# Splitting a broadcast load into two DMAs of 64 partitions, with a list schedule's constants set anew

## The chip, the cores and the metric

The kernel runs on one core of a Trainium2 chip. The core has five engines, each working through its own queue in order: TensorE (matrix products, PE in the profile, with its weight loads as PEld), VectorE (DVE), ScalarE (ACT), GpSimd (POOL) and SyncE (SP, which here only issues DMAs). Sixteen DMA engines move data between HBM and the on-chip memory. The metric is the device time of one execution in microseconds.

## The reference

Three layers stand in series. The change lies in the first.

```python
def phi(x):                                     # features, 64 -> 2 * 128
    proj = np.einsum('bhsd,df->bhsf', x, w_phi)
    proj = proj - np.max(np.abs(proj), axis=-1, keepdims=True)
    return np.concatenate([np.exp(proj), np.exp(-proj)], axis=-1)
q_p, k_p = phi(q), phi(k)                       # q, k, v: (4, 8, 576, 64)
kv = np.einsum('bhsf,bhsd->bhfd', k_p, v)
z = np.sum(k_p, axis=2)
num = np.einsum('bhsf,bhfd->bhsd', q_p, kv)
den = np.einsum('bhsf,bhf->bhs', q_p, z)[..., None] + 1e-06
x = num / den                                   # -> 2304 tokens x 512
h = np.maximum(x @ w_in, 0); x = h * h @ w_out  # 512 -> 2048 -> 512
# then a layer of 8 experts (512 -> 1024 -> 512), each weighted per token by
# a softmax of x @ w_gate that is normalised 8 times along rows and columns
```

`w_in` and `w_out` arrive as 64-bit floats. The kernel reads them as pairs of 32-bit integers and decodes them on VectorE.

## The kernel before

**Attention.** The 4 x 8 heads are handled as 16 units of two heads each (NU = 16; unit `u` is batch `u // 4` and head pair `u % 4`). The two heads of a unit lie on partitions 0 to 63 and 64 to 127. The steps of a unit, with their names in the planner: loads of k, q and v (`ldk`, `ldq`, `ldv`, SP); transposes (`tk`, `tq`, TensorE) and copies (`kc`, `qc`, ScalarE); the feature projection of k (`pk`), its peak and shift (`mkp`, `mkr`, `sup`, `sur`, VectorE) and the two exponentials (`en`, `ep`, ScalarE); the sums over the tokens (`A`, TensorE), a copy and a transpose (`kvs`, `kvt`), `kvc` and the reduction for z (`zs` on VectorE, `zw`, a copy, on GpSimd); the same features for q in two halves (`pq`, `ec`, the absolute maximum over all partitions `par` on GpSimd, `qs`, `qn`, `qp`); the numerators `psn` and the denominators `psd` (TensorE).

**The reciprocal and its way.** A unit has 2 x 576 denominators. `dn` (ScalarE) copies them out of the accumulator, `cmp` (a DMA) spreads them over 128 partitions with 9 each, `rec` (VectorE) takes the reciprocals, `rd` (a DMA) writes them to a small array `rden` in HBM, and `rb` (a DMA) reads them back so that each partition of a head holds all 576 values of that head. The source of this DMA is 2 heads x 64 copies (step 0) x 576 values, and the target 128 partitions. `mul` (VectorE) multiplies the numerators by them. `xhi` (GpSimd) and `xlo` (VectorE) split the product into a high and a low part, `xh` and `xl`, the input of the next layer. The tile `rb` exists once, so `rb` of a unit waits for `mul` of the unit before.

**The first pass of the second layer** is mixed into the same stage. Its weights are decoded in 12 blocks of 7 VectorE steps (`op`; blocks 0, 2, 4 and 6 for the first pass, two tiles each, 8 to 15 for the second, one tile each) and split (`sh`, `sl`). Of its eight groups of 288 tokens, six have their first product (`L1`) in the plan and five their second (`L2`); results go to HBM (`od`, the store `part<-o`). Each of these products is 12 matmuls, since a product of two split numbers takes three.

**What sets the order.** Lines 287 to 397 are a list scheduler that runs on the host when the kernel is built. Each step has an engine, a duration (us), the steps that it needs, the accumulator banks that it takes and frees, and a key. The scheduler goes through time; on each engine it picks, of the steps that are ready, the one with the smallest key. The key of an attention step is its unit's base, `EARLY * min(u, 5) + LATE * max(0, u - 5)`, plus `PHASE[name]`; that of a decode block is `DUE[block]` (first loads: `RAW`); the products of the second layer have keys of 10,000 and more, so they fill what is left; steps with no key get their ready time plus `SOON`. DMAs are priced as one issue (`ISSUE`, 0.63 us), 1 us, `kb / 195` us (in order, one after another) and 0.25 us. The scheduler's result fixes only the order in which each engine's instructions are issued. The times on the chip come from the hardware.

Nearly all instructions of the stage are recorded through two helpers, so that they carry line 104 (VectorE, ScalarE, GpSimd and SP) or line 224 (TensorE); tile names tell them apart. `psw`, `pss`, `pskt` are accumulators of the attention, `ps` of the second layer; `ek` and `eq` are features of k and q, `nm` the numerators, `dm` and `wf` tiles of the decode.

**After the stage** come the rest of the first pass, three further passes and the expert layer. None of their code is touched.

Of the kernel before, what the change touches and what calls it, by code (L numbers as in the profile page):

```python
# [20 lines left out]
def tile_features_attention__moe__sinkhorn_moe(  # L21
# [20 lines left out]
    B, H, S, D = q.shape  # L42
# [3 lines left out]
    NE, _, FE = w1.shape  # L46
# [25 lines left out]
    ep = early.enter_context(tc.tile_pool(name="early", bufs=1, side="right", reuse_waits="tile"))  # L72
# [7 lines left out]
    rden = dram.tile([NU, T2], F32, name="rden")  # L80
# [30 lines left out]
    A = InOrder(nc.scalar, "act")  # L111
# [157 lines left out]
    def first_l2(g, t0, n, dst=None, pool=None, cols=range(KD)):  # L269
# [15 lines left out]
    S_ = InOrder(nc.sync, "sp")  # L285

    LAT = {"PE": 0.30, "DVE": 0.07, "ACT": 0.07, "POOL": 0.10, "SP": 0.07}
    RINGS = {"w": 2, "s": 2, "m": 2}
    EARLY, LATE = 12.97, 18.72
    PHASE = {  # L290
        "ldk": -41.9, "ldq": -26.4, "ldv": -12.4, "tq": 0.3, "qc": -8.6, "tk": -5.8, "kc": -29.8, "pk": 1.3,
        "mkp": -19.8, "sup": -1.2, "mkr": -3.5, "sur": -14.7, "en": -3.0, "ep": -6.7, "A": 4.4, "kvs": 20.1,
# [3 lines left out]
        "rb": 13.8, "mul": 6.0, "xhi": 38.2, "xlo": 39.8, "ldw": -30.9,  # L296
    }
    START = {"PE": 2.2, "DVE": 2.2, "ACT": 3.0, "POOL": 9.0, "SP": 0.8}

    ISSUE = 0.63  # L300
    SOON = 1.33
    SLACK = {"PE": 0.4, "DVE": 0.1, "ACT": 0.1, "POOL": 0.1, "SP": 0.0}
    FREELY = "ws"
    class Step:
# [8 lines left out]
    def add(name, eng, dur, emit, needs=(), after=(), takes=(), frees=(), key=0.0, kb=0, cols=0):  # L313
        steps[name] = Step(
            name, eng, dur, emit, [n for n in needs if n], [n for n in after if n], takes, frees, key, kb, cols
        )

    def schedule():
# [34 lines left out]
        while len(made) < len(steps):  # L353
# [30 lines left out]
            for u, whole in s.users:  # L384
                u.ready = max(u.ready, s.end if whole else s.start)
                u.left -= 1
                if u.key is None:
                    u.key = s.end + SOON
                if not u.left:
# [10 lines left out]
    def attention(u):  # L400
# [3 lines left out]
        def n(nm, v=u):  # L404
            return f"{nm}{v}" if 0 <= v < NU else None
# [3 lines left out]
        def step(nm, *args, **how):  # L409
            add(n(nm), *args, key=base + PHASE[nm], **how)  # L410
# [50 lines left out]
        def k_peak(c):  # L461
            def emit():
                ps = x["ps" + c]
                mk = x["mk", c] = ab.tile([P, ps.shape[1], 1], F32, tag="mk" + c, bufs=1, name="mk")
                V.tensor_reduce(mk, ps, AX.X, ALU.max, apply_absolute_value=True)

            return emit

        def k_shift(c):
            def emit():  # L470
                if c == "p":
                    x["ek"] = ab.tile([P, 2 * MT + 1, 2, NF], F32, tag="ek", bufs=1, name="ek")
                ps, ek = x["ps" + c], x["ek"]
                to = ek[:, : 2 * MT, 0] if c == "p" else ek[:, 2 * MT :, 0]
                V.tensor_sub(to, ps, x["mk", c].to_broadcast(list(ps.shape)))

            return emit

        def k_exp(sign):
            ek = x["ek"]  # L480
            A.activation(ek[:, :, 1 if sign < 0 else 0], ek[:, :, 0], AF.Exp, scale=float(sign))

        step("pk", "PE", 1.15, proj_k, [n("kc"), "ldw"], [n("A", u - 1)], ("w", "s"), ([n("sup")], [n("sur")]), cols=2)
        step("mkp", "DVE", 1.23, k_peak("p"), [n("pk"), n("sup", u - 1)])
        step("mkr", "DVE", 0.29, k_peak("r"), [n("pk"), n("sur", u - 1)])
        step("sup", "DVE", 1.23, k_shift("p"), [n("mkp"), n("A", u - 1)])
        step("sur", "DVE", 0.29, k_shift("r"), [n("mkr"), n("sup"), n("A", u - 1)])
        step("en", "ACT", 1.02, lambda: k_exp(-1), [n("sup"), n("sur")])
        step("ep", "ACT", 1.02, lambda: k_exp(1), [n("en")])

        def rows(i, h):
            return x["ek"][:, 2 * MT if i == MT else MT * h + i].rearrange("p a f -> p (a f)")
# [42 lines left out]
        step("kvt", "PE", 0.40, kvt, [n("kvs")], [], ("m",), ([n("kvc"), n("zs")],))  # L535
        step("kvc", "ACT", 0.37, kvc, [n("kvt"), n("psn", u - 1)])
        step("zs", "DVE", 0.17, zs, [n("kvt"), n("zw", u - 1)])
        step("zw", "POOL", 0.44, zw, [n("zs"), n("psd", u - 1)])

        x["psq"] = [None, None]  # L540

# [26 lines left out]
        def of(function, *args):  # L568
            return lambda: function(*args)

        for c in range(2):
            step(f"pq{c}", "PE", 0.52, of(proj_q, c), [n("qc"), "ldw"], [n("psd", u - 2)], ("w",), ([n(f"ec{c}_")],), cols=2)
            step(f"ec{c}_", "ACT", 0.64, of(q_copy, c), [n(f"pq{c}"), n("psn", u - 2), n("psd", u - 2)])
            step(f"par{c}_", "POOL", 2.26, of(q_peak, c), [n(f"ec{c}_")])
            step(f"qs{c}_", "DVE", 0.85, of(q_shift, c), [n(f"par{c}_")])
            step(f"qn{c}_", "ACT", 0.68, of(q_exp, c, -1), [n(f"qs{c}_")])
            step(f"qp{c}_", "ACT", 0.68, of(q_exp, c, 1), [n(f"qn{c}_")])
# [42 lines left out]

        def to_rows():
            t = x["rb"] = ab.tile([P, S], F32, tag="rb", bufs=1, name="rb")
            S_.dma_start(t, rden[u].rearrange("(j o s) -> j o s", j=2, o=1).to_broadcast([2, D, S]))

        ts_ = slice(b * S, (b + 1) * S)

# [11 lines left out]
        )  # L638
        step("psd", "PE", 1.13, denominators, [n("qp0_"), n("qp1_"), n("zw")], [n("psn")], ("s",), ([n("dn")],), cols=1)
        step("nm", "ACT", 0.65, nm, [n("psn"), n("xlo", u - 2), n("xhi", u - 2)])  # L640
        step("dn", "ACT", 0.4, dn, [n("psd"), n("cmp", u - 1)])
        step("cmp", "SP", ISSUE, to_comp, [n("dn"), n("rd", u - 1)], kb=20)
        step("rec", "DVE", 0.22, recip, [n("cmp")])
        step("rd", "SP", ISSUE, to_dram, [n("rec")], kb=20)
        step("rb", "SP", ISSUE, to_rows, [n("rd"), n("mul", u - 1)], kb=230)
        step("mul", "DVE", 0.83, mul, [n("rb"), n("nm")])
        raws_of = []
        step("xhi", "POOL", 1.0, xhi, [n("mul")] + raws_of)
        step("xlo", "DVE", 0.86, xlo, [n("xhi")] + raws_of)

    def load_wphi():
        S_.dma_start(wphi, w_phi.rearrange("(o d) f -> o d f", o=1).to_broadcast([2, D, NF]))
# [2 lines left out]
    for u in range(NU):  # L655
        attention(u)

    def decoding(j, wide):
# [37 lines left out]
        for d in range(c):  # L696
            add(
                f"ldr{j + d}", "SP", ISSUE, load(d),
                [f"ldr{j + d - 1}" if j + d else None, f"op{prev}_5" if j == 6 or j > 8 else None]
                + (["ldq0"] if j + d == 0 else []) + [], key=RAW.get(j, due - 5) + d / 10, kb=512,  # L700
            )
# [18 lines left out]
            add(f"sh{j}", "ACT", 1.05, sh, [f"op{j}_6"], key=due + 8)  # L720
            add(f"sl{j}", "DVE", n / 960 + 0.15, sl, [f"sh{j}"], key=due + 9)

    RAW = {0: -31.09, 2: -7.57, 4: 30.41, 6: 29.03}
    DUE = {
        0: 19.8, 2: 58.2, 4: 67.3, 6: 90.9, 8: 117.7, 9: 126.3, 10: 134.8, 11: 143.4, 12: 151.9, 13: 160.5,
        14: 169.0, 15: 177.6,
    }
    for j in range(0, 8, 2):
        decoding(j, True)
# [609 lines left out]
    for n in range(NN):  # L1339
        l2 = layer2(n)  # L1340
        if n + 1 < NN:
            l1 = layer1(n + 1)
            p, q = order[n + 1]
# [75 lines left out]
```

## Time and profile before

| | |
|---|---|
| median of 3 runs (range) | 2108.54 us (2107.21 to 2110.11) |
| profiled execution: time, span | 2110.18 us, 2108.4 us |
| TensorE busy | 2040.1 us (97%) |
| VectorE, ScalarE, GpSimd busy | 1670.2, 827.9, 810.8 us |
| mean granted TensorE clock | 0.986 |
| DMA | 375.12 MB, mean 178 GB/s |

The span runs from the first to the last instruction. All times in rows are microseconds from the span's start, or durations, unless they say ns. "Busy" of TensorE is the time in which matmuls are in flight by a model of their ends. PEclk is the granted clock as a share of full speed, 1.00 being 2.4 GHz. In a group's row, what stands after the bar is the time that the engine sat idle just before such instructions, with what ended most of it. The chain of waits is followed back from the last instruction, at each step to what released it; "SPq" is SP's queue.

### The profile page before, as it was taken

What the parts mean: (1) busy time and instruction counts of PE and PEld (TensorE: products, weight loads), DVE (VectorE), ACT (ScalarE), POOL (GpSimd) and SP (SyncE); (2) the same over time, 40 slices, a digit from 0 to 9 for tenths busy, and PEclk for the clock granted to TensorE, in tenths of its full rate; (3) what the DMA queues carried; (4) which work ended last, traced back from release to release, by engine and by line L of the source; (5) the groups of instructions that cost most, each with busy time, mean ns of one, the idle gap of its engine ahead of it and who ended that gap; (6) DMA issues with size and microseconds to landing.
All of it is one profiled execution on the core that took longest, in us unless ns stands there. A gap on an engine that the chain in (4) does not pass through costs nothing.

```text
span 2108.4 us, 31244 instructions
## 1 busy us (share of the span) xinstructions
PE 2040.1 (97%) x12427; PEld 1922.3 (91%) x12427; DVE 1670.2 (79%) x1910; ACT 827.9 (39%) x1240; POOL 810.8 (38%) x457
## 2 busy tenths in 40 slices
PE   7888879999999999999999999999999999999998
PEld 4466559888899999999999999999999999999998
DVE  6657433757456798999989989889898998988986
ACT  5655433222233654333433334333333333333332
POOL 3323310323102644443544444444444444444431
PEclk9889989999999999999999999999999999999999
DMA  5434213101134566667676676676766666676663
GB/s 146 102 97 111 73 38 94 61 30 51 40 123 169 228 225 216 215 219 253 222 229 220 215 252 223 222 232 214 243 226 225 229 222 231 224 229 233 212 202 121
DMA packets 180643, 375.12 MB, mean 178 GB/s; under 512 B 71058, under 2 KB 110866, under 8 KB 180498
## 3 DMA queue, kind: packets, MB, share of 16 engines
q1 hardware_dynamic: 180498, 373.12, 53.2%
q8 instruction: 99, 1.62, 0.3%
q14 instruction: 46, 0.38, 0.1%
HBM read 348.67 MB, written 24.34 MB: 177 GB/s over the span
## 4 chain that ended last, share of the span: by engine, by line
PE 84%; DMA 7%; DVE 6%; issue 1%; SPq 1%; ACT 1%; POOL 0%; DVEq 0%; ACTq 0%; POOLq 0%
PE psa L1160 31%; PE psb L1160 31%; PE ps L224 18%; DMA rb<-rden 5%; PE psw L224 2%; PE pss L224 2%; SPq L104 1%; DMA xl<-xv 1%; DVE acc L1276 1%; DVE xl L896 1%; PE psg L937 1%; DVE r L1228 0%; DVE w2v L896 0%; DVE nm L104 0%; DMA rden<-comp 0%
## 5 line engine op out<-in xcount | busy, mean ns | idle before, releaser
L1160 PE MATMUL psa<-xl,xh 128*128 128x384 f32 x2400 | 447.0, 335 | 3.6 <-DVE xl L896 2.5
L1160 PE MATMUL psb<-xl,xh 128*128 128x384 f32 x2400 | 445.0, 334 | 2.0 <-DVE acc L1276 0.7
L1160 PEld LDWEIGHTS psa<-xl,xh 128*128 128x128 f32 x2400 | 419.7, 188 | 4.7 <-DVE xl L896 2.9
L1160 PEld LDWEIGHTS psb<-xl,xh 128*128 128x128 f32 x2400 | 418.1, 188 | 3.2 <-issue 1.7
L1188 POOL TENSOR_TENSOR t<-r,r 128x768 f32<-128x768 f32 x96 | 207.1, 2157 | 503.7 <-DVE r L1228 457.9
L1188 POOL TENSOR_TENSOR t<-r,t 128x768 f32<-128x768 f32 x96 | 236.0, 2458 | 7.4 <-ACT r L1232 1.9
L896 DVE TENSOR_TENSOR xl<-t,xl 128x768 fp32r<-128x768 f32 x128 | 186.8, 1460 | 1.9 <-ACT xl L895 1.7
L1276 DVE TENSOR_TENSOR acc<-psa,acc 128x768 f32<-128x768 f32 x161 | 152.9, 950 | 40.0 <-PE psa L1160 36.4
L1276 DVE TENSOR_TENSOR acc<-psb,acc 128x768 f32<-128x768 f32 x163 | 154.8, 950 | 37.0 <-PE psb L1160 33.7
L1160 PE MATMUL psb<-xl,w2v 128*128 128x384 f32 x960 | 180.3, 334 | 0.0
L1160 PE MATMUL psa<-xl,w2v 128*128 128x384 f32 x960 | 180.2, 334 | 0.0
L895 ACT CAST xl<-t 128x768 fp32r<-128x768 f32 x128 | 107.1, 837 | 155.5 <-POOL t L1188 65.5
L1160 PEld LDWEIGHTS psb<-xl,w2v 128*128 128x128 f32 x960 | 167.6, 188 | 0.0
L1160 PEld LDWEIGHTS psa<-xl,w2v 128*128 128x128 f32 x960 | 167.6, 188 | 0.0
L895 ACT CAST xl<-r 128x768 fp32r<-128x768 f32 x96 | 80.4, 838 | 155.8 <-PE psa L1160 79.2
L224 PE MATMUL ps<-xh,w0h 128*128 128x288 f32 (+3 forms) x384 | 133.9, 349 | 4.1 <-ACT o L104 3.8
L896 DVE TENSOR_TENSOR xl<-r,xl 128x768 fp32r<-128x768 f32 x96 | 132.4, 1379 | 1.4 <-ACT xl L895 1.4
L224 PE MATMUL ps<-xl,w0h 128*128 128x288 f32 (+3 forms) x384 | 131.5, 342 | 0.0
L224 PE MATMUL ps<-xh,w0l 128*128 128x288 f32 (+3 forms) x384 | 131.2, 342 | 0.0
L224 PE MATMUL ps<-gl,w1h 128*128 128x288 f32 (+3 forms) x384 | 129.5, 343 | 0.0
L224 PE MATMUL ps<-gh,w1l 128*128 128x288 f32 (+3 forms) x384 | 128.6, 341 | 0.0
L969 POOL TENSOR_TENSOR s<-wf 128x512 f32<-128x512 f32 x32 | 44.6, 1393 | 212.6 <-DVE xvs L896 80.6
(198 smaller groups left out, 3585.7 us busy)
## 6 DMA issues: line engine op xcount, KB each, us to landing
xl<-xv SPq DMA_DIRECT2D x329, 768.0 KB
wf<-in_moe_w_dram SPq DMA_DIRECT2D x32, 1024.0 KB
gate<-prT SPq DMA_DIRECT2D x45, 384.0 KB
xv<-xvs SPq DMA_DIRECT2D x14, 768.0 KB
raw<-in_moe_w_in_dram SPq DMA_DIRECT2D x16, 512.0 KB
raw<-in_moe_w_out_dram SPq DMA_DIRECT2D x16, 512.0 KB
xv<-xl SPq DMA_DIRECT2D x7, 768.0 KB
rb<-rden SPq DMA_DIRECT2D x16, 288.0 KB
```

Of the source, the lines that this page charges most:

```text
L104: ins = made(*args, **how)
L224: latest["pe"] = op(*args, **how).ins
L895: nc.scalar.copy(v[:, 0], src)
L896: nc.vector.tensor_sub(v[:, 1], src, v[:, 0].bitcast(F32))
L937: ins = nc.tensor.matmul(ps[:, t], accT[:, k, t0 + t * P : t0 + (t + 1) * P], wg[:, k], start=first is None, stop=k == KD - 1, skip_group_ ...
L969: nc.gpsimd.tensor_tensor(s1, a(2, 1), a(2, 2), ALU.add)
L1160: ins = nc.tensor.matmul(ps[:, x, :NB], w[:, wi, k, cs], b[:, bi, k], start=first and k + i == 0, stop=k == KH - 1 and i == 2, skip_group_ ...
L1188: nc.gpsimd.tensor_tensor(t[nm], x, y, ALU.subtract)
L1276: latest["dve"] = nc.vector.tensor_add(o, ps, o).ins
```

## The change

The load of `rb` becomes two DMAs, one per head, each with 64 target partitions and a source of 64 copies x 576 values. Its planned duration becomes two issues. Nothing else that is executed changes; durations, keys and spacings of the planner do, and with them the order of instructions on the engines in the attention stage.

```diff
-    EARLY, LATE = 12.97, 18.72
+    EARLY, LATE = 17.72, 18.72
     PHASE = {                       # nearly every entry changes; those around the reciprocal:
-        "qp1_": 13.6, "psn": -16.0, "psd": 20.6, "nm": 14.8, "dn": 4.3, "cmp": 21.7, "rec": 10.9, "rd": 16.7,
-        "rb": 13.8, "mul": 6.0, "xhi": 38.2, "xlo": 39.8, "ldw": -30.9,
+        "qp1_": 13.7, "psn": -29.8, "psd": 23.7, "nm": 18.5, "dn": 4.2, "cmp": 4.3, "rec": 7.7, "rd": 22.4,
+        "rb": 26.1, "mul": 12.8, "xhi": 31.6, "xlo": 31.8, "ldw": -33.0,
...
-    SOON = 1.33
+    SOON = 1.67
...
-        step("pk", "PE", 1.15, ...
+        step("pk", "PE", 1.30, ...
-        step("sup", "DVE", 1.23, ...
+        step("sup", "DVE", 1.21, ...
-        step("en", "ACT", 1.02, ...            # ep likewise
+        step("en", "ACT", 1.16, ...
-        step("zw", "POOL", 0.44, ...
+        step("zw", "POOL", 0.48, ...
-            step(f"pq{c}", "PE", 0.52, ...
+            step(f"pq{c}", "PE", 0.58, ...
...
         def to_rows():
             t = x["rb"] = ab.tile([P, S], F32, tag="rb", bufs=1, name="rb")
-            S_.dma_start(t, rden[u].rearrange("(j o s) -> j o s", j=2, o=1).to_broadcast([2, D, S]))
+            for j in range(2):
+                S_.dma_start(t[j * D : (j + 1) * D], rden[u, j * S : (j + 1) * S].rearrange("(o s) -> o s", o=1).to_broadcast([D, S]))
...
-        step("dn", "ACT", 0.4, ...
+        step("dn", "ACT", 0.48, ...
-        step("rb", "SP", ISSUE, to_rows, [n("rd"), n("mul", u - 1)], kb=230)
+        step("rb", "SP", 2 * ISSUE, to_rows, [n("rd"), n("mul", u - 1)], kb=230)
-        step("xlo", "DVE", 0.86, ...
+        step("xlo", "DVE", 0.93, ...
...
-    RAW = {0: -31.09, 2: -7.57, 4: 30.41, 6: 29.03}
+    RAW = {0: -31.04, 2: -7.65, 4: 27.29, 6: 15.82}
     DUE = {
-        0: 19.8, 2: 58.2, 4: 67.3, 6: 90.9, 8: 117.7, 9: 126.3, 10: 134.8, 11: 143.4, 12: 151.9, 13: 160.5,
-        14: 169.0, 15: 177.6,
+        0: 14.2, 2: 62.0, 4: 72.2, 6: 93.5, 8: 116.9, 9: 125.0, 10: 133.1, 11: 141.2, 12: 149.3, 13: 157.3,
+        14: 165.4, 15: 173.5,
```

## Rows read from the trace of the kernel before

**Rows 1.** Stretches: span, PE, PEld, DVE, ACT, POOL busy (instructions), PEclk, DMA share, GB/s.

```profile
0.00:318.00 318.00, 261.47 (x2227) 178.47 (x2228) 179.11 (x285) 167.31 (x280) 94.06 (x85) 0.93 0.36 95
20.00:318.00 298.00, 249.91 (x2141) 170.76 (x2140) 173.79 (x277) 158.93 (x269) 87.39 (x65) 0.92 0.34 91
333.00:2108.00 1775.00, 1763.62 (x10103) 1728.82 (x10101) 1487.43 (x1617) 656.02 (x949) 716.77 (x372) 1.00 0.57 193
```

**Rows 2.** Chain of waits, 0 to 330 us: shares by line; start, duration, what.

```profile
by line: DMA rb<-rden 30.9%; PE ps L224 12.0%; PE psw L224 11.1%; PE pss L224 10.1%; SPq L104 5.7%; issue 4.1%; DVE nm L104 2.6%; DMA rden<-comp 2.6%; DMA part<-o 2.3%; DVE mk L104 2.0%; DVE ek L104 1.8%; DVE wf L104 1.6%; DVE xl L104 1.6%;
...
37.87 8.82 DMA rb<-rden
...
171.50 8.98 DMA rb<-rden
...
187.69 3.93 DMA rden<-comp
```

**Rows 3.** A stretch in which only `rb` moves; columns as in rows 1.

```profile
312.50:315.30 2.80, 0.03 (x1) 0.00 (x0) 0.00 (x0) 0.00 (x0) 0.00 (x0) 0.97 0.12 45
```

**Rows 4.** DMA issues of the page: what, how many, KB each.

```profile
rb<-rden SPq DMA_DIRECT2D x16, 288.0 KB
...
rden<-comp SPq DMA_DIRECT2D x16, 4.5 KB
```

**Rows 5.** Chain of waits, 284 to 320 us.

```profile
287.44 1.40 DMA rden<-comp
...
288.86 8.03 DMA rb<-rden
...
308.19 7.63 DMA part<-o
```

**Rows 6.** Timeline of SP's queue: start, time on the queue, issue.

```profile
149.49 0.97 SPq L104 DMA_DIRECT2D nq<-in_q_dram  x2
```

**Rows 7.** Groups, 0 to 330 us: busy us, mean ns | idle before, releasers.

```profile
L104 POOL PARTITION_ALL_REDUCE eq<-eq x32 | 70.7, 2216 | 100.4 <-ACT eq L104 100.4
...
L104 ACT ACTIVATE ek<-ek 128x1152 f32<-128x1152 f32 x32 | 37.3, 1166 | 33.8 <-DVE ek L104 33.5
...
L104 DVE SCALAR_TENSOR_TENSOR wf<-raw,wf 128x512 f32<-128x512 uint32 (+1 forms) x12 | 12.3, 1029 | 0.3
L104 DVE TENSOR_TENSOR nm<-nm,rb 128x576 f32<-128x576 f32 x16 | 12.1, 758 | 77.5 <-DMA rb<-rden 77.5
...
L104 POOL COPY z<-zs 128x128 f32<-128x128 f32 x16 | 8.3, 521 | 12.3 <-DVE zs L104 12.2
```

**Rows 8.** Timeline of TensorE, three of its pauses: start, duration, what [idle before <-releaser].

```profile
50.22 2.16 PE L224 MATMUL psw<-eq,kv 128*64 128x288 f32 x16 [2.71 <-ACT eq L104]
...
80.16 1.12 PE L224 MATMUL pskt<-ident,kvs 128*128 128x128 f32 x4 [4.89 <-ACT kvs L104]
...
316.38 0.61 PE L224 MATMUL ps<-xh,w0h 128*128 128x288 f32 x1 [3.84 <-ACT o L104]
```

**Rows 9.** Shorter stretches; columns as in rows 1.

```profile
0.00:20.00 20.00, 11.56 (x88) 7.71 (x88) 5.33 (x9) 8.38 (x12) 6.67 (x20) 1.00 0.60 154
...
60.00:100.00 40.00, 31.92 (x259) 18.16 (x258) 28.39 (x38) 21.91 (x34) 15.31 (x10) 0.83 0.47 116
100.00:140.00 40.00, 35.52 (x289) 25.03 (x287) 25.97 (x46) 22.70 (x41) 12.06 (x8) 0.87 0.33 83
...
300.00:318.00 18.00, 14.16 (x91) 13.01 (x82) 3.65 (x8) 3.77 (x9) 0.91 (x4) 0.78 0.15 49
```

**Rows 10.** The projection's matmuls (tile `wphi`): ns least/median/most, first and last start.

```profile
L224 PE MATMUL psw<-wphi,kT x256: 272/272/576, 7.3 to 276.0; 64*128 64x128 f32 x128
```

**Rows 11.** A stretch, instructions on tile `dm` alone: DVE, POOL busy, PEclk, DMA share, GB/s.

```profile
0.00:330.00 330.00, 50.73 (x72) 0.00 (x0) 0.92 0.37 99
```

**Rows 12.** Chain of waits, 180 to 200 us, between two transfers `rb`.

```profile
183.59 0.69 DVE dm L104
...
186.87 0.12 DVE comp L104
```

More of the change, by code (lines that the diff above doesn't have):

```diff
@@ L288, in tile_features_attention__moe__sinkhorn_moe @@
     RINGS = {"w": 2, "s": 2, "m": 2}
-    EARLY, LATE = 12.97, 18.72
+    EARLY, LATE = 17.72, 18.72
     PHASE = {
-        "ldk": -41.9, "ldq": -26.4, "ldv": -12.4, "tq": 0.3, "qc": -8.6, "tk": -5.8, "kc": -29.8, "pk": 1.3,
-        "mkp": -19.8, "sup": -1.2, "mkr": -3.5, "sur": -14.7, "en": -3.0, "ep": -6.7, "A": 4.4, "kvs": 20.1,
[3 rows of a table removed]
-        "rb": 13.8, "mul": 6.0, "xhi": 38.2, "xlo": 39.8, "ldw": -30.9,
+        "ldk": -37.2, "ldq": -14.9, "ldv": 2.3, "tq": -5.0, "qc": -9.2, "tk": -8.1, "kc": -32.3, "pk": 13.2,
+        "mkp": -10.2, "sup": -3.5, "mkr": -6.2, "sur": -15.6, "en": 13.3, "ep": -6.7, "A": 2.4, "kvs": 15.3,
[3 rows of a table added]
+        "rb": 26.1, "mul": 12.8, "xhi": 31.6, "xlo": 31.8, "ldw": -33.0,
     }
@@ L481, in k_exp @@
             A.activation(ek[:, :, 1 if sign < 0 else 0], ek[:, :, 0], AF.Exp, scale=float(sign))
-        step("pk", "PE", 1.15, proj_k, [n("kc"), "ldw"], [n("A", u - 1)], ("w", "s"), ([n("sup")], [n("sur")]), cols=2)
+        step("pk", "PE", 1.30, proj_k, [n("kc"), "ldw"], [n("A", u - 1)], ("w", "s"), ([n("sup")], [n("sur")]), cols=2)
         step("mkp", "DVE", 1.23, k_peak("p"), [n("pk"), n("sup", u - 1)])
         step("mkr", "DVE", 0.29, k_peak("r"), [n("pk"), n("sur", u - 1)])
-        step("sup", "DVE", 1.23, k_shift("p"), [n("mkp"), n("A", u - 1)])
+        step("sup", "DVE", 1.21, k_shift("p"), [n("mkp"), n("A", u - 1)])
         step("sur", "DVE", 0.29, k_shift("r"), [n("mkr"), n("sup"), n("A", u - 1)])
-        step("en", "ACT", 1.02, lambda: k_exp(-1), [n("sup"), n("sur")])
-        step("ep", "ACT", 1.02, lambda: k_exp(1), [n("en")])
+        step("en", "ACT", 1.16, lambda: k_exp(-1), [n("sup"), n("sur")])
+        step("ep", "ACT", 1.16, lambda: k_exp(1), [n("en")])
         def rows(i, h):
@@ L537, in attention @@
         step("zs", "DVE", 0.17, zs, [n("kvt"), n("zw", u - 1)])
-        step("zw", "POOL", 0.44, zw, [n("zs"), n("psd", u - 1)])
+        step("zw", "POOL", 0.48, zw, [n("zs"), n("psd", u - 1)])
         x["psq"] = [None, None]
@@ L571, in attention @@
         for c in range(2):
-            step(f"pq{c}", "PE", 0.52, of(proj_q, c), [n("qc"), "ldw"], [n("psd", u - 2)], ("w",), ([n(f"ec{c}_")],), cols=2)
+            step(f"pq{c}", "PE", 0.58, of(proj_q, c), [n("qc"), "ldw"], [n("psd", u - 2)], ("w",), ([n(f"ec{c}_")],), cols=2)
             step(f"ec{c}_", "ACT", 0.64, of(q_copy, c), [n(f"pq{c}"), n("psn", u - 2), n("psd", u - 2)])
@@ L640, in attention @@
         step("nm", "ACT", 0.65, nm, [n("psn"), n("xlo", u - 2), n("xhi", u - 2)])
-        step("dn", "ACT", 0.4, dn, [n("psd"), n("cmp", u - 1)])
+        step("dn", "ACT", 0.48, dn, [n("psd"), n("cmp", u - 1)])
         step("cmp", "SP", ISSUE, to_comp, [n("dn"), n("rd", u - 1)], kb=20)
@@ L648, in attention @@
         step("xhi", "POOL", 1.0, xhi, [n("mul")] + raws_of)
-        step("xlo", "DVE", 0.86, xlo, [n("xhi")] + raws_of)
+        step("xlo", "DVE", 0.93, xlo, [n("xhi")] + raws_of)
     def load_wphi():
```

4 rows, old and new, of the table PHASE are left out of this document.

## The prediction

> **What bounds the kernel now.** I read the busy time by stages first [rows 1]. From 333 us to the end TensorE is busy 1763.6 of 1775 us at a granted clock of 1.00; the change touches nothing there, so that stretch can only move as a block. Between 20 and 318 us, the stage that the planner orders, it is busy 249.9 of 298 us: 48.1 us idle, at a mean clock of 0.92. VectorE (179.1 us of 318), ScalarE (167.3) and GpSimd (94.1) are far from full. So what the change can win is idle TensorE time and low clock in the first 318 us.
>
> Second, the chain of waits over the first 330 us [rows 2]. Its largest item is no engine but the transfer `rb<-rden`: 30.9%, in 12 pieces of 8.03 to 8.98 us, 101.9 us together, where TensorE's three largest lines make 33.2% (12.0 + 11.1 + 10.1). Sixteen such transfers are issued, one per unit; twelve lie on the chain.
>
> Third, why a transfer of 288 KB takes 8 us [rows 3 to 5]. From 312.5 to 315.3 us `rb` moves alone: the DMA share is 0.12 and the rate 45 GB/s. 0.12 of 16 engines is two engines, 23 GB/s each. The long stretch from 333 us moves 193 GB/s at a share of 0.57, 21.2 GB/s per busy engine: nothing is slow about the two, there are only two. 294,912 bytes at 45 GB/s are 6.55 us; the quietest piece took 8.03, so 1.48 us are fixed, and the 4.5 KB transfer `rden<-comp` beside it took 1.40. The source of `rb` has the two heads as outermost dimension, which fits the two engines.
>
> **The transfer, before and after.** Each new DMA has 64 partitions outermost. If each spreads over 16 engines at 21.2 GB/s (339 GB/s), one half of 147 KB needs 0.43 us. The second is issued one issue later: the load of q, already two DMAs of one step, occupies SP's queue for 0.97 us [rows 6], so 0.5 us each, with 0.1 to the next; I take 0.65. Landing after the first issue: 0.65 + 0.43 + 1.48 = 2.6 us against 8.03 in the quiet case, 5.5 us earlier; against the mean of the chain's twelve pieces, 101.9 / 12 = 8.5, it is 5.9. I use 5.7. Bounds: where `rden<-comp` ran beside a load it took 3.93 instead of 1.40 [rows 2, 5]; 2.5 us of such queueing on top leave 3.2 us gained. The other bound is no gain at all, the third rival.
>
> Twelve pieces by 5.7 are 68 us on the chain. That is a ceiling which something else cuts, so I count it at TensorE.
>
> **What the wait does to TensorE.** VectorE works in order, and the multiplication that needs `rb` keeps it idle 77.5 us over 16 waits [rows 7]. Behind that multiplication stand the peak and shift of the next k features and the reduction for z; behind those the exponentials, GpSimd's copies and TensorE. In the timeline I looked for TensorE pauses above 0.5 us that end within 7 us after such a multiplication starts (for the last, after the transfer lands) [rows 8]: 16 pauses, from 2.71 us at 50.22 to 3.84 us at 316.38, together 43.1 of the stage's 48.1 us. None is over 4.9, so 5.7 us covers each. The last one shows a side effect [rows 5]: the store `part<-o`, issued after `rb`, landed only after 7.63 us at 315.82, 0.4 us after `rb`, because it stood behind it on the shared engines; ScalarE waited for that store, and TensorE for ScalarE.
>
> What is late next: GpSimd's absolute maxima (2216 ns, two per unit, 70.9 us of its time), VectorE's decode and the exponentials (two of 1166 ns per unit) [rows 7] were partly hidden in the same pauses. The bounds are 0 and 43.1 us; most pauses end on a short step held up only by queue order (a copy of z, 0.5 us), so I take 70%: 30 us.
>
> **The clock.** The granted clock is 0.83 from 60 to 100 us and 0.87 from 100 to 140, the first of these with the pause of 4.89 us in it; it is 0.78 from 300 to 318, where TensorE is idle 3.84 of the 18 us [rows 9]. At 0.92 over 298 us, (1 - 0.92) x 2 x 298 = 48 us run at 1.2 instead of 2.4 GHz. A 64x128 projection takes 272 ns in the median and 576 at most in the stage [rows 10], so at most half, 24 us, comes back if no pause is left. I take a third, 8 us, with 0 and 24 as bounds.
>
> **The new keys and durations.** Corrected durations (0.02 to 0.15 us a step) are not executed; they only reorder. The spacing of the first five units grows from 12.97 to 17.72, so unit 5 and all later units get keys 23.75 us later, while the last decodes become due up to 4.1 us earlier: for VectorE the decode moves ahead by about 1.4 units. The trace shows no such order. Above, a gain is bounded by the pauses I did not count, 48.1 - 43.1 = 5 us. Below, all decode work on VectorE is 50.7 us with the tile `dm` and 12.3 us in the one form without it, 63 us [rows 7, 11], and at worst none of it is hidden any more. I take 0: VectorE has 318 - 179 = 139 us idle, and loses 77.5 of that wait at the same time. SP issues 16 DMAs more, 16 x 0.65 = 10 us. Behind them stand the next unit's loads and the next `cmp`; SP's issues do hold 5.7% of the chain, 18.8 us [rows 2], but those stand ahead of an `rb`, and the new one stands behind its first half, where it delays the landing by the 0.65 us counted above. So 0 more, and at most 10 us if each also delayed what follows.
>
> **Sum.** 30 + 8 = 38 us off the profiled execution's own 2110.2 us (span 2108.4 and 1.8 around it): 2072.2. The median of the runs is 1.6 us below that execution, so I predict 2071 us. By bounds: 43 + 5 + 24 = 72 us off gives 2037; 12 us off gives 2097.
>
> **Rivals.**
>
> 1. *The cover returns (15%).* `rb` lands early but the pauses are refilled: GpSimd's two maxima per unit, or decode, become what TensorE waits for. For it: GpSimd is busy 94 us, mostly in 2.2 us pieces, and a k feature step still passes VectorE, ScalarE and TensorE in series. Against it: GpSimd idles 100 us just before those maxima, waiting for ScalarE's copies [rows 7]. Then only the tail (its 3.8 us pause) and some 20% of the other 39 us stay: 3.8 + 7.9 = 12 us, 2097.
>
> 2. *More than I count (10%).* All pauses go and most of the low clock: 43 + 17 = 60 us, 2048. For it: the chain's ceiling is 68. Against it: TensorE's first 20 us are only 11.6 busy, and that start does not change.
>
> 3. *The halves do not spread (5%).* If each DMA still moves with two engines, landing stays near 8.5 us and the second issue adds 0.65: 12 x 0.65 = 8 us, 2116. The split itself then costs. Against it: two engines fit the two heads, and the DMA share reaches 0.60 in a stretch of 128-partition loads [rows 9].
> The Trainium skill, "DMA: Bandwidth & Descriptors", section "Rules for kernel authors", speaks for this rival: two transfers to disjoint partition halves gain nothing, it says, because both spread over all 16 engines and serialize; one transfer of 128 partitions is better. By that rule alone the result is the 2116 of this rival. The trace disagrees with its premise: the existing transfer holds 0.12 of the engines. Another row of the same section says that an outermost dimension below 16 confines a DMA to that many engines, and with 0.12 the trace agrees.
>
> 4. *The order is worse: slower (9%).* Decode, ahead by 1.4 units, is put in front of a peak, a shift or `rec` that TensorE's chain needs. Price: up to 63 us; the point from which it decides is 38 us, three fifths of the decode. With 45 us of it on the chain the time is 2108.5 - 38 + 45 = 2116. For it: in the chain before, decode already holds up `rec` between two `rb` (a decode step before the reciprocal, and the next `rden<-comp` only then) [rows 12]. Against it: a block is seven separate steps, between which others fit; 12 blocks of 7 share the 63 us, 0.75 us a step.
>
> **How the numbers follow.** The forecast has 60%; its own range is 2056 to 2086 (70 us of pauses and clock at shares of 30 to 80%). The range for 8 in 10 is 2044 to 2100: outside are half of rival 2, a little of rival 1, and rivals 3 and 4. 0.2% is 4.2 us, about what a measurement tells from no change. Faster: forecast 60, rival 2 10, rival 1 14, and a case of rival 4 in which decode eats only part, 1: 85%. Same: 1 each of rivals 1 and 3, 3 of rival 4: 5%. Slower: 4 of rival 3, 5 of rival 4, 1 left over: 10%.
>
> **What would show it.** Right: `rb` lands within about 3 us of its first issue, with a DMA share well over 0.12 while it moves alone; VectorE's idle time before the multiplication falls from 77.5 us to under 30; `rb` drops off the top of the chain; TensorE's idle time between 20 us and the stage's end falls by about 30 us and the clock there rises above 0.92; the stretch from 333 us keeps its length and shifts by the whole gain. Wrong: a landing near 8 us (rival 3); an early landing but pauses that end on `eq`, `z` or decode (rivals 1 and 4); or a later stretch that grows by what the first stage wins.

## The result and the profile after

The changed kernel takes 2052.8 us (median of 4 runs, 2051.98 to 2053.61) against 2107.88 us before in the same comparison: a ratio of 0.9738, 95% interval 0.9721 to 0.9755. That is 55 us less where 37 to 38 were forecast.

The page after, span and busy time:

```profile
span 2050.2 us, 31276 instructions
...
PE 2019.9 (99%) x12427; PEld 1906.3 (93%) x12427; DVE 1674.1 (82%) x1910; ACT 827.4 (40%) x1240; POOL 812.8 (40%) x457
```

Set against the page before (2108.4 and 2040.1 us), this splits the 58.2 us of span in two: TensorE's idle time falls from 68.3 to 30.3 us (38.0), and the same 12,427 matmuls are in flight for 20.2 us less. By stretches, the same rows as [rows 1], with each limit moved by 57.2 us, the shift of the later work (the first matmul into `psa` starts at 624.2 instead of 681.4 us):

```profile
20.00:260.80 240.80, 230.77 (x2126) 155.99 (x2121) 175.96 (x275) 157.76 (x267) 87.17 (x61) 0.99 0.43 110
275.80:2050.20 1774.40, 1762.10 (x10115) 1727.29 (x10113) 1488.07 (x1617) 656.38 (x950) 717.89 (x372) 1.00 0.57 193
```

The late stretch keeps its length (1775 and 1774.4 us). In the planned stage the idle time is 10.0 us instead of 48.1, and the clock 0.99 instead of 0.92. The chain of waits over the first 340 us, for [rows 2]:

```profile
by line: PE ps L224 36.6%; PE psw L224 22.8%; PE pss L224 19.0%; PE pskt L224 2.5%; DMA rb<-rden 2.0%; ACT eq L104 1.8%; DVE dm L104 1.8%; SPq L104 1.8%; issue 1.4%; DVE eq L104 1.4%; ACT ek L104 1.3%; DMA wphi<-in_w_phi_dram 1.3%; DVE wf L
...
40.55 3.33 DMA rb<-rden
52.48 3.57 DMA rb<-rden
```

Twelve pieces of `rb` became two, and TensorE's lines now hold the chain. The transfer by tile (issues on SP's queue in ns; issue to landing in us, where the three equal figures stand for the one landing that the view can time, that of the second DMA of a pair), and the multiplication's group, for [rows 7]:

```profile
L104 SPq DMA_DIRECT2D rb<-rden x32: 451/560/602, 39.9 to 262.1; - x32
...
DMA to landing us min/median/max: 3.0/3.0/3.0
```

```profile
L104 DVE TENSOR_TENSOR nm<-nm,rb 128x576 f32<-128x576 f32 x16 | 14.3, 895 | 2.2 <-DMA rb<-rden 2.2
```

VectorE waits 2.2 us for the transfer, not 77.5.

### The profile page after: what moved, and what is told of

Same layout as the page of the kernel before. It is cut to its first block, busy times and chain, and to the rows that moved or that the text cites. A ratio compares the mean times of both kernels' runs of the same rounds, so it can differ in the third digit from the quotient of the medians.

```text
span 2050.2 us, 31276 instructions
## 1 busy us (share of the span) xinstructions
PE 2019.9 (99%) x12427; PEld 1906.3 (93%) x12427; DVE 1674.1 (82%) x1910; ACT 827.4 (40%) x1240; POOL 812.8 (40%) x457
## 4 chain that ended last, share of the span: by engine, by line
PE 92%; DVE 4%; DMA 2%; ACT 1%; issue 1%; SPq 0%; POOL 0%; DVEq 0%; ACTq 0%; POOLq 0%
PE psa L1161 32%; PE psb L1161 32%; PE ps L224 19%; PE psw L224 4%; PE pss L224 3%; DMA xl<-xv 1%; PE psg L938 1%; DVE acc L1277 1%; DVE xl L897 1%; PE pskt L224 0%; DVE acc L1307 0%; DVE xh L897 0%; DVE hv L897 0%; DMA rb<-rden 0%; DVE r L1229 0%
```

## The experiments

Every ratio below is to the kernel before, with its 95% interval.

**The split alone.** The kernel before, planner constants and order as they were, with the new `to_rows`.

```diff
-            S_.dma_start(t, rden[u].rearrange("(j o s) -> j o s", j=2, o=1).to_broadcast([2, D, S]))
+            for j in range(2):
+                S_.dma_start(t[j * D : (j + 1) * D], rden[u, j * S : (j + 1) * S].rearrange("(o s) -> o s", o=1).to_broadcast([D, S]))
```

> The kernel before with the split alone: two DMAs of 64 partitions, all durations, keys and spacings of the planner as before, so the order of instructions as before but for one more DMA per unit. Theory T1 (the transfer was confined to two DMA engines, and its landing time is what the change sells): rb lands about 3 us after its first issue instead of 8.4, VectorE's idle time before the multiplication drops from 77.5 to under 25 us, most of the 43 us of TensorE pauses go: 2060 to 2080 us. Theory T2 (the new order hides the wait, the split does little): 2095 to 2108 us.

Measured: 2045.28 us, ratio 0.9699 (0.9682 to 0.9717). T2 falls, and T1 was too timid: the split alone wins more than the whole change. Its page, the planned stage and the multiplication's group:

```profile
span 2044.7 us, 31272 instructions
...
PE 2019.4 (99%) x12427; PEld 1906.5 (93%) x12427; DVE 1675.5 (82%) x1910; ACT 827.8 (40%) x1240; POOL 813.1 (40%) x457
```

```profile
20.00:255.50 235.50, 228.57 (x2145) 154.43 (x2142) 176.91 (x275) 158.20 (x267) 87.70 (x61) 1.00 0.44 114
```

```profile
L104 DVE TENSOR_TENSOR nm<-nm,rb 128x576 f32<-128x576 f32 x16 | 14.7, 916 | 17.0 <-DMA rb<-rden 16.9
```

The span is 63.7 us shorter: 43.0 us less idle TensorE (68.3 to 25.3), 20.7 us less busy at a clock of 1.00. VectorE still waits 17 us for the transfer, but TensorE is idle for only 6.9 us of the stage (235.5 - 228.6).

**The new order alone.** The changed kernel with `rb` as one DMA again (the diff above reversed).

> The changed kernel with its new planner constants, but rb again as one DMA with the two heads outermost. T1: the landing stays near 8.4 us, VectorE idles 60 us or more before the multiplication, and the time is 2090 to 2125 us (the new order puts the multiplication where a transfer of 3 us has landed, so it may be worse than before). T2: 2053 to 2070 us.

Measured: 2103.86 us, 0.9974 (0.9962 to 0.9986), as T1 expected. VectorE still waits for the transfer:

```profile
L104 DVE TENSOR_TENSOR nm<-nm,rb 128x576 f32<-128x576 f32 x16 | 12.1, 758 | 60.7 <-DMA rb<-rden 60.7
```

`rb` holds 30.9% of the first 340 us of the chain, in 12 pieces with a mean of 8.8 us. With the slow transfer the new constants are worth about 5 us; with the fast one they cost 7.5.

**Same halves, outermost dimension 2.** The changed kernel, each half's source written as 2 x 32 copies.

```diff
-                S_.dma_start(t[j * D : (j + 1) * D], rden[u, j * S : (j + 1) * S].rearrange("(o s) -> o s", o=1).to_broadcast([D, S]))
+                S_.dma_start(t[j * D : (j + 1) * D], rden[u, j * S : (j + 1) * S].rearrange("(a o s) -> a o s", a=1, o=1).to_broadcast([2, D // 2, S]))
```

> The changed kernel, still two DMAs of 64 partitions each, but each source written as 2 x 32 copies instead of 64, so the outermost dimension of the source is 2. Bytes, rows, targets and order are unchanged. T1 in the form 'the outermost dimension of the source sets the number of engines': each half holds two engines; if both halves get the same two, landing is about 8.5 to 9 us and the time that of the new order with one DMA, within 10 us; if they get different ones, about 5 us. Rival T3 (two DMAs of 64 partitions are faster because they are two, or because a half fits better): as the changed kernel, 2050 to 2056 us.

Measured: 2128.55 us, 1.0107 (1.0077 to 1.0136). A stretch in which little but `rb` moves, and the multiplication's group:

```profile
314.00:321.00 7.00, 6.26 (x56) 4.42 (x55) 0.72 (x2) 2.72 (x6) 0.30 (x1) 1.00 0.13 37
```

```profile
L104 DVE TENSOR_TENSOR nm<-nm,rb 128x576 f32<-128x576 f32 x16 | 12.1, 758 | 84.3 <-DMA rb<-rden 84.3
```

Same bytes, same targets, same two DMAs as in the changed kernel, 76 us slower: T3 falls. A share of 0.13 is two engines, although two DMAs of two engines each are open: both halves got the same two. I had expected a time within 10 us of the new order with one DMA; it is 25 us above. The 13 pieces on the chain (mean 9.6 us, counted from the second issue) land some 1.5 us later, and VectorE waits 84.3 us instead of 60.7, about as much as the kernel lost.

**Outermost dimension 4.** The split with the old order, each source written as 4 x 16 copies.

```diff
-                S_.dma_start(t[j * D : (j + 1) * D], rden[u, j * S : (j + 1) * S].rearrange("(o s) -> o s", o=1).to_broadcast([D, S]))
+                S_.dma_start(t[j * D : (j + 1) * D], rden[u, j * S : (j + 1) * S].rearrange("(a o s) -> a o s", a=1, o=1).to_broadcast([4, D // 4, S]))
```

> The split with the old order, but each source written as 4 x 16 copies, so that its outermost dimension is 4. If the outermost dimension sets the number of engines and both halves share the same four, the data need 295 KB / (4 x 22 GB/s) = 3.4 us and land about 5 to 5.5 us after the first issue, against 8.9 to 11.4 with 2 x 32 and 2.9 to 5.1 with 64: VectorE idles 30 to 45 us before the multiplication and the time is 2055 to 2075 us. If the outermost dimension does not matter beyond 2, as the split with 64: 2043 to 2048 us.

Measured: 2070.81 us, 0.9821 (0.9806 to 0.9836), as the first theory said. The landing is a little later than expected: the chain holds 11 pieces of `rb` with a mean of 5.8 us from the second issue, where 5 to 5.5 from the first were expected. A stretch in which no other transfer has been issued, and the group:

```profile
263.00:265.00 2.00, 1.54 (x13) 1.29 (x13) 0.00 (x0) 0.79 (x2) 0.00 (x0) 1.00 0.26 79
```

```profile
L104 DVE TENSOR_TENSOR nm<-nm,rb 128x576 f32<-128x576 f32 x16 | 14.1, 879 | 46.0 <-DMA rb<-rden 46.0
```

0.26 of 16 is four engines. In the old order an outermost dimension of 2 (one DMA), 4 and 64 (two DMAs each) thus gives 77.5, 46.0 and 17 us of VectorE's wait, and about 2108, 2071 and 2045 us: roughly 1 us of time per us of wait.

**No transfer.** The changed kernel without `rb`: the numerators are multiplied by a constant tile, so the division is left out.

```diff
-            t = x["rb"] = ab.tile([P, S], F32, tag="rb", bufs=1, name="rb")
-            for j in range(2):
-                S_.dma_start(...)
+            x["rb"] = flat
```

> The changed kernel without the transfer rb: the numerators are multiplied by a constant tile instead of the reciprocals, so the division by the denominator is left out; everything up to the store to HBM is kept, and so is the order. If what is left of the transfer's latency still delays TensorE (the chain gives rb 2.4% of the first 290 us, 7 us), 2045 to 2050 us; if it is hidden, 2051 to 2054 us.

Measured: 2051.05 us, 0.9725 (0.9706 to 0.9744); the interval overlaps that of the changed kernel. What is left of the transfer is hidden: taking away the two pieces on the chain gains at most about 2 us.

**Which constants cost the 7.5 us?** First, are they real? Both kernels once more, in five rounds on one chip.

> The split with the old order once more, in five rounds beside the changed kernel on the same chip: is the old order really faster under the split? If it is, 2043 to 2048 us and 5 us or more below the changed kernel; if the 7.5 us were scatter between chips, within 4 us of it.

> The changed kernel once more, in five rounds beside the split with the old order: 2051 to 2055 us if the new constants cost what the first runs show.

Measured: the split with the old order 2044.17 us, 0.9685 (0.9672 to 0.9699); the changed kernel 2051.63 us, 0.9721 (0.9708 to 0.9734). The 7.5 us stand. Then parts of the new constants were set back in the changed kernel.

```diff
-    EARLY, LATE = 17.72, 18.72
+    EARLY, LATE = 12.97, 18.72
```

> The changed kernel with only the spacing of the first five units set back to 12.97. The split with the old order is 7.5 us faster than the changed kernel; which of the constants costs that? Theory O1 (the spacing: later units lie 24 us behind the decode's due times, so decode gets ahead of them on VectorE): 2044 to 2049 us, with the low clock between 60 and 100 us gone. Theory O2 (the phases within a unit): 2050 to 2056 us.

Measured: 2065.67 us, 0.9798 (0.9784 to 0.9813). The low clock between 60 and 100 us is not gone but lower, 0.83. Next, the table of phases alone:

```diff
-    PHASE = {"ldk": -37.2, ...}     # the new table
+    PHASE = {"ldk": -41.9, ...}     # the old table
```

> The changed kernel with only the table of phases set back. O2 (the phases within a unit: the copy kvs stands behind the exponentials of q on ScalarE, and TensorE's transposes wait for it, 2.5 us at 63 us): 2044 to 2049 us, and no TensorE pause on kvs. O1: 2050 to 2056 us. If neither this nor the spacing alone brings it back, the constants act only together.

Measured: 2058.55 us, 0.9766 (0.9751 to 0.978). TensorE's pauses on `kvs` did shrink, as O2 expected. They were 2.9 us together in the changed kernel, the longest 2.5; here (us in total, times, longest):

```profile
PE pskt L224 <- ACT kvs L104: 0.8, 3, 0.4
```

The time rose all the same. Both together:

> The changed kernel with spacing and phases both set back; due times of the decode, first loads, durations and the lead SOON stay new. Each of the two alone made it slower (2066 and 2059 us against 2053). Theory O3 (spacing and phases belong together, and together they are what costs 7.5 us): 2043 to 2049 us. Rival O4 (every mixture of the two sets is worse than either set, because each was found as a whole): 2053 to 2070 us.

Measured: 2057.18 us, 0.9747 (0.9734 to 0.9761). Last, the durations and `SOON` alone:

```diff
-        step("rb", "SP", 2 * ISSUE, ...
+        step("rb", "SP", ISSUE, ...      # and the other eight durations, and SOON 1.33
```

> The changed kernel with only the planned durations and SOON set back (they are nowhere executed). O4 (mixtures are worse): 2055 to 2070 us, though each duration moves by 0.63 us at most. If durations decide little: 2050 to 2055 us.

Measured: 2053.41 us, 0.9725 (0.9711 to 0.9738): the durations decide little. O1, O2 and O3 fall. O4 fits the three kernels with spacing or phases set back, each of which is slower than either whole set; the one with old durations is as fast as the changed kernel. The kernel with spacing and phases both set back differs from the split with the old order only in the decode's due times, the first loads, the durations and `SOON`: under old spacing and phases the new ones cost 2057 - 2044 = 13 us. Which order of which two instructions does it is not settled.

**wphi, the other load with two heads outermost.** The split with the old order, and:

```diff
-        S_.dma_start(wphi, w_phi.rearrange("(o d) f -> o d f", o=1).to_broadcast([2, D, NF]))
+        for j in range(2):
+            S_.dma_start(wphi[j * D : (j + 1) * D], w_phi)
```

> The split with the old order, and the load of wphi at the start (64 KB, one DMA with a source of 2 x 64 rows) split into two DMAs of 64 partitions as well. The first projection waits 1.8 us for it, and its other operand (the copy of kT) is ready about 6.4 us after the start, wphi at 7.3: the wait shrinks by 0.5 to 1 us and the kernel by as much, 2044 to 2045 us, which the timing alone can't tell from no change.

Measured: 2046.28 us, 0.9701 (0.9683 to 0.9719), no difference in time. The first projection starts at 6.24 us instead of 7.34 in the split with the old order. It then waits 0.73 us for `kT`, no longer 1.78 us for `wphi`; a microsecond is below what these runs tell apart. The fastest version is the split with the old order, measured twice (2045.3 and 2044.2 us).

## Why the prediction was right, and where its sizes were off

**What bounds the kernel: right.** The gain lies wholly in the planned stage, and is idle TensorE time and low clock as the first view said.

**Two engines: right, and shown.** In two pairs of kernels the outermost dimension is the only difference: 2 and 64 in the new order (2128.55 and 2052.8 us), 4 and 64 in the old one (2070.81 and 2045.28 us). Outermost dimensions of 2 and 4 give shares of 0.13 and 0.26. With 64 there is a stretch of the changed kernel in which only `rb`, issued at 250.31 us, moves:

```profile
252.00:253.00 1.00, 0.91 (x8) 0.68 (x6) 0.00 (x0) 0.15 (x1) 0.00 (x0) 1.00 0.64 210
```

That is ten engines on average, as the prediction asked for (well over 0.12 alone). The split in two counts for nothing by itself. Rival 3's condition was therefore the right one to name, and its price too small: I gave 8 us, and the kernel whose halves do not spread is 25 us above the new order with one DMA.

**Landing: 1 us or more late, at little cost.** I worked out 2.6 us after the first issue. The one landing that can be timed came 3.0 us after the second issue, so about 3.6 after the first; the two pieces on the chain (3.33 and 3.57 us, beside other loads) began with the second issue and ended 4.0 and 4.2 us after the first. Part of this is the fixed term of 1.48 us. The stretch of [rows 3] also holds the end of the store `part<-o`, which landed only at 315.82 us, so its 45 GB/s are not those of `rb` alone. From 292 to 295 us, where nothing else had been issued, the kernel before shows a share of 0.13 and 49 GB/s. At 49 GB/s the data need 6.0 us, and 2.0 of the 8.03 are fixed. VectorE's wait of 2.2 us and the kernel without `rb` show that this lateness costs at most about 2 us. The same kernel has none of SP's additional issues, which I took at 0, so they cost no more than that either.

**TensorE's pauses: the share was too small.** I counted 43.1 us of pauses behind the multiplication and took 70%, 30 us. The split alone removes 43.0 us of idle time from the whole span, the whole change 38.0. Counted as in the prediction, pauses behind the multiplication, 43.1 us become 0.7 (one pause) in the changed kernel and 2.8 (four) with the split alone: nearly all of it went, not 70%. The stage's other pauses were 5.0 us before and are 9.3 and 4.1. Rival 1 (the cover returns) does not appear: GpSimd's 32 maxima take 74.2 us (70.7 before), and no TensorE pause of the stage ends on GpSimd.

**The clock: the term that was most mis-sized.** I took a third of the 24 us, 8; the busy time fell by 20.2 us (20.7 with the split alone). Of the 48 us at 1.2 GHz some 7 are left in the changed kernel, all in the stretch from 60 to 100 us (0.91), and with the split alone none in the stage. Most of the bound of 24 us came back; from 20 us on, no TensorE pause above 2.5 us is left in the changed kernel's stage.

**The new order: taken at 0, it is a loss.** It costs 7.5 us with the fast transfer. In these two kernels' traces the loss lies between 20 and 100 us. First the changed kernel, then the split with the old order (columns as in [rows 1]):

```profile
20.00:60.00 40.00, 35.84 (x351) 20.68 (x345) 36.02 (x47) 27.47 (x42) 17.18 (x11) 1.00 0.54 136
60.00:100.00 40.00, 34.90 (x306) 22.75 (x306) 35.37 (x49) 27.55 (x45) 18.76 (x13) 0.91 0.50 134
```

```profile
20.00:60.00 40.00, 37.76 (x376) 21.87 (x373) 35.42 (x47) 29.57 (x46) 18.15 (x11) 1.00 0.49 129
60.00:100.00 40.00, 37.28 (x363) 22.75 (x362) 35.65 (x49) 29.14 (x46) 19.16 (x12) 1.00 0.52 130
```

TensorE is busy 70.7 instead of 75.0 us there, and 7 us run at 1.2 GHz, worth half: 4.3 + 3.6 = 7.9 us, more than the 5.5 us between the two spans (2050.2 and 2044.7). In the repeated pair TensorE is busy 70.3 against 75.0 us there, with a clock of 0.96 from 60 to 100 us: 4.7 + 1.6 = 6.3 of the 8.1 us between those spans. One link of the changed kernel's chain is what rival 4 described, decode in front of a shift that TensorE needs, though small:

```profile
58.01 1.48 DVE dm L104
59.49 1.78 DVE eq L104
...
62.69 0.48 ACT kvs L104
63.21 1.12 PE pskt L224 x4
```

A step of the decode, the shift of q, two exponentials and the copy `kvs` stand in series, and TensorE pauses 2.49 us. That this link is the cause is not shown, and two runs speak against it. With the phases set back the longest pause on `kvs` is 0.4 us and the time 2058.55 us. With the durations set back there is no such pause, and the stretch from 20 to 100 us is nearly as good as with the split alone:

```profile
20.00:100.00 80.00, 74.13 (x725) 44.36 (x723) 73.52 (x100) 59.89 (x94) 37.59 (x24) 1.00 0.51 131
```

Yet that kernel takes 2053.41 us. It loses later: from 100 to 300 us TensorE is busy 195.2 us, against 198.0 with the split alone. Each order pays at other places, and why the new sets are slower stays open; the nearest that the runs come is the 13 us of the new due times, first loads and durations under the old spacing and phases.

**The sum.** Forecast 30 + 8 + 0 = 38; measured 43.0 + 20.7 = 63.7 for the transfer, and about 7.5 given back by the order. The mechanism held. The measured 2052.8 us lies in the range for 8 in 10 (2044 to 2100) but below the forecast's own range (2056 to 2086), 4.8 us from the 2048 of rival 2, to which I gave 10%, and 18 us from my 2071. That it came as near as 18 us is in part luck: the two terms of the transfer were 25.7 us too small together, and the order, taken at 0, gave 7.5 of that back. The forecast's own range was also added up wrongly: 30 to 80% of 70 us off 2108.6 us are 2053 to 2088.

## What to carry to other kernels

Look at the DMA share while one transfer moves alone: share times 16 is the number of engines at work, and if it equals the outermost dimension of the source, the access pattern and not the bytes sets the time. When one wait is behind nearly all pauses of the bounding engine, count the pauses and the low clock behind them in full before discounting them, for here nearly all of both went. When a transfer is mended and a schedule set anew in one step, time the mend alone: here it was 7.5 us better without the rest. And before a pause in the trace is called the cause of a loss, look for a run without it: here the loss stayed when the pause went.

## What the runs showed of the hardware beyond that

Two DMAs that are each confined to two engines shared the same two (share 0.13, 37 GB/s with both open), so splitting without changing the outermost dimension makes the landing later. Another transfer issued right behind the confined one lands late though most engines are free. In the kernel before, a 144 KB store behind `rb` took 7.63 us [rows 5]. With four engines, the store issued 0.1 us behind the last pair took 5.87 us (at 275.33 us on the chain), where the median of the store's timed landings is 1.7. In the kernel with the split alone, no timed landing of it is above 3.1 us.
